# Splitting the value product of a fused FNet + SwiGLU kernel inside one accumulator bank, on ten of twelve units of a tile

## The chip, the cores and the metric

The kernel runs on one core of one Trainium2 chip. The metric is device time in microseconds (us) of one execution; the time of a kernel is the median over its timed runs. Beside the timed runs there is one profiled execution, whose trace gives every instruction of the five engines: PE (TensorE, the matmuls), DVE (VectorE), ACT (ScalarE), POOL (GpSimd) and SP (SyncE, which here only issues DMAs).

## The reference

```python
# x: (8, 3008, 256) float32; w_gate, w_val: (256, 1536); w_out: (1536, 256)
X = np.fft.fft(x, axis=1)
X = np.fft.fft(X, axis=2)
x = X.real.astype(np.float32).reshape(24064, 256)
g = x @ w_gate
silu = g * (1.0 / (1.0 + np.exp(-g)))
val = x @ w_val
out = (silu * val @ w_out).astype(np.float32)      # (24064, 256)
```

## The kernel before

The 24,064 rows of the Fourier transform come in mirrored pairs: row k and row M-k of a batch share an even part P (in the tile `Pt`) and an odd part Q (in `Qt`). The kernel never forms the rows. It multiplies P and Q with weights that hold the second Fourier transform already (`Wp`, `Wq`, and `Wm`, which is minus two times `Wq` in all rows but the first). So P·Wp + Q·Wq is the value for row k, and adding Q·Wm to that turns it into the value for the mirrored row. In the rest of this text "plus" is row k and "minus" is the mirrored row.

The 12,032 pairs lie in 24 tiles (`wide`): tiles 0 and 3 have 480 columns, tile 23 has 320, the others 512. Each tile has 12 units, one for each block of 128 hidden columns (`f`), so there are 288 units `(t, f)`, done in order by the loop at L954. A unit needs a gate and a value for both signs:

- `part_a(u)` (L761) opens a bank `g` of PSUM for the gate and adds P·Wp and Q·Wq into it (two matmuls, helper at L771).
- In a **whole** unit the value bank `v` gets the same two matmuls; ACT takes silu(g) into `sg` (L808), and DVE multiplies it with `v` into `hp`, the plus half of the hidden tile (L809). In the next unit, `part_b(prev)` (L812) adds Q·Wm to both banks (two matmuls, L818); ACT takes silu again (L826) and DVE multiplies into `hm`, reversed (L827). That is six matmuls, two silus and two DVE instructions.
- In a **split** unit the value bank `e` gets P·Wp alone. DVE adds the first row's term (L787: `es = bc*w0 + e`, `bc` being a broadcast of row 0 of Q). The inner function `odd()` (L789), run after four output matmuls of the same unit, puts Q·Wm into a second bank `o` (one matmul); DVE makes the plus value `es - o/2` into a buffer `VV` (L793) and the minus value `es + o/2`. POOL multiplies the plus value with silu(g) into `hp` (L800). In kind "P" the minus value goes into `VV` too, reversed (L796), and POOL makes `hm` (L823). In kind "H" the minus value stays in PSUM (L799) and DVE makes `hm` (L827). `part_b` then adds Q·Wm to the gate only. That is five matmuls, two silus, and for "P" three DVE and two POOL instructions, for "H" four DVE and one POOL.

`split(u)` (L754) looks the kind up in four tables. Tile 0 has no split unit, tile 1 five, tile 2 six, tiles 3 to 18 seven each (f = 0, 2, 10 of kind H; 4, 6, 8, 9 of kind P), tiles 19 to 22 eight each (all P), tile 23 seven.

Between these matmuls stand the output matmuls of the tile before (`OWork`, L707; L734): 96 of 256 columns for a 512-column tile, eight in each unit, in two groups of four. ACT copies their banks out (L694) and SP sends the rows. The next batches' P and Q are made in the same loop: POOL folds the input (L167 to L198, spread over the units by `seq`), and at two neighbouring units (f = 4 and 5 of a tile) `transform` (L579) runs matmuls into one `v` and one `g` bank, ACT copies one (L619), and DVE adds the two into `Pt` and `Qt` ("puts", L624).

PSUM has eight banks: three for `g`, three for `v` and `e`/`o` and the transform, two for the output. They come from rotating pools (L78 to L80), as do the SBUF buffers `sg` (3), `sgv` (4) and `es` (2); `VV` has four slots in turn. The order of the instructions on each engine is the order in which the code writes them.

Of the kernel before, what the change touches and what calls it, by code (L numbers as in the profile page):

```python
# [12 lines left out]
F32 = mybir.dt.float32  # L13
# [18 lines left out]
def kernel(  # L32
# [8 lines left out]
    nc = tc.nc  # L41
# [33 lines left out]
    cp = ctx.enter_context(tc.tile_pool(name="coef", bufs=2))  # L75
    pqp = ctx.enter_context(tc.tile_pool(name="pq", bufs=5))
    odp = ctx.enter_context(tc.tile_pool(name="od", bufs=2))
    psG = ctx.enter_context(tc.tile_pool(name="psG", bufs=3, space=bass.MemoryType.PSUM))  # L78
    psV = ctx.enter_context(tc.tile_pool(name="psV", bufs=3, space=bass.MemoryType.PSUM))
    psO = ctx.enter_context(tc.tile_pool(name="psO", bufs=2, space=bass.MemoryType.PSUM))  # L80
    ctx.enter_context(tc.manual_schedule())

    Wp = const.tile([P, 2, Dff], BF16, name="Wp")
    Wq = const.tile([P, 2, Dff], BF16, name="Wq")
# [494 lines left out]
    def transform(b, part, eos, given=None):  # L579
        n = NCE if part == 0 else G  # L580
        ev, ods = {}, {}
        ps = given or {eo: [pool.tile([P, T], F32, name=nm) for pool, nm in ((psV, "v"), (psG, "g"))] for eo in eos}

        def product(eo, kind, q, coef, r, qc, ch, start):
            CE, BB = coef
            if part == 0:
                cols = KINDS[kind][1]
                l, r_ = ce_main(CE, r, qc, eo, kind), Tab[r, ch, q, eo, cols]
            else:
                cols = slice(0, G)  # L590
                l, r_ = BB[r, qc, eo, kind, 0:P], Tab[r, ch, q, (eo + kind) % 2, NOO:NTAB]
            nc.tensor.matmul(ps[eo][q][:, cols], l, r_, start=start, stop=(ch == 1 and kind == 1), skip_group_check=True)  # L592

        if not given:
            every = slice(0, P)
            for eo in eos:
                for q in range(2):
                    for kind in range(2):
                        product(eo, kind, q, coef_a(b), every, q, 0, kind == 0)
                    if part == 0 and eo == 1:  # L600
                        row0(coef_a(b)[0], every, q, 0, q, ps[eo][q])
            for eo in eos:
                for kind in range(2):
                    for q in range(2):
                        if b == 0:
                            product(eo, kind, q, coef_c(b), every, q, 1, False)
                        else:
                            product(eo, kind, q, coef_c(b), half(q), b % 2, 1, False)
                if part == 0 and eo == 1:
                    for kind, cols in KINDS:  # L610
                        for q in range(2):
                            r = half(q)
                            nc.tensor.matmul(ps[eo][q][:, cols], ce_zero(coef_c(b)[0], r, b % 2, kind),
                                             Tab[r, 1, q, 0, cols], start=False, stop=True, skip_group_check=True)
        for q in range(2):
            for eo in eos:
                if q == 0:
                    ods[eo] = odp.tile([P, NCE], F32, name="od")
                    nc.scalar.copy(ods[eo][:, 0:n], ps[eo][q][:, 0:n])  # L619
                else:  # L620
                    ev[eo] = ps[eo][q]

        def put(eo, dst, s0, w, minus):
            nc.vector.tensor_tensor(dst, ev[eo][:, s0:s0 + w], ods[eo][:, s0:s0 + w],  # L624
                                    op=Alu.subtract if minus else Alu.add)

        if part == 0:
            runs = [(0, GH, 1, 0), (GH, GH, 0, 1), (G, GH, GH + 1, 0), (G + GH, GH, GH + 1, 1)]
        else:
            runs = [(2 * G, G, 0, 0), (3 * G, G, 0, 1)]  # L630
        todo = []
        for eo in eos:
            for c0, n_, s0, minus in runs:
                for t, off, src, w in pieces(b * H + c0, n_):
                    todo.append((t, eo, off, s0 + src, w, minus))
        for t, eo, off, s0, w, minus in sorted(todo, key=lambda v: v[0:2]):
            put(eo, pq_tiles(t)[eo][:, off:off + w], s0, w, minus)
        if part == 0:
            for eo in eos:
                put(eo, last[eo][:, b:b + 1], 0, 1, 0)  # L640
# [13 lines left out]


    hp = ctx.enter_context(tc.tile_pool(name="ht", bufs=2))
    sgp = ctx.enter_context(tc.tile_pool(name="sg", bufs=3))
    rdp = ctx.enter_context(tc.tile_pool(name="rd", bufs=2, space=bass.MemoryType.DRAM))
    sgv = ctx.enter_context(tc.tile_pool(name="sgv", bufs=4))
    esp = ctx.enter_context(tc.tile_pool(name="es", bufs=2))  # L660
    bcp = ctx.enter_context(tc.tile_pool(name="bc", bufs=2))

# [80 lines left out]
    owork = None  # L743

    ROW0 = (7, 9)
    SPLIT = {0: "H", 2: "H", 4: "P", 6: "P", 8: "P", 9: "P", 10: "H"}
    SPLIT_END = {0: "P", 1: "P", 3: "P", 4: "P", 6: "P", 8: "P", 9: "P", 11: "P"}
    SPLIT_1 = {2: "H", 4: "P", 6: "H", 8: "P", 10: "H"}
    SPLIT_2 = {0: "H", 2: "H", 4: "P", 6: "P", 8: "H", 10: "H"}
    t_end = tile_of((B - 1) * H) - 1  # L750

    bc = {}
# [1 line left out]
    def split(u):  # L754

        t, f = u
        if t == 0 or (t == nT - 1 and f > 9):
            return None
        return (SPLIT_1 if t == 1 else SPLIT_2 if t == 2 else SPLIT if t < t_end else SPLIT_END).get(f)

    def part_a(u):  # L761
        t, f = u
        n = width(t)
        w = n + (B if t == nT - 1 else 0)
        fs = slice(f * P, (f + 1) * P)
        if f == 0:
            hts[t] = (hp.tile([P, nF, T + B], BF16, name="hp"), hp.tile([P, nF, T], BF16, name="hm"))
        Pt, Qt = pq_tiles(t)

        def mm(ps, Wt, gv, src, start, stop):  # L770
            nc.tensor.matmul(ps[:, :w], Wt[:, gv, fs], src[:, :w], start=start, stop=stop,  # L771
                             skip_group_check=True)

        g = psG.tile([P, T], F32, name="g")
        mm(g, Wp, 0, Pt, True, False)
        if u == (0, 0):
            v = psV.tile([P, T], F32, name="v")
            mm(v, Wp, 1, Pt, True, False)
        mm(g, Wq, 0, Qt, False, True)
        if split(u):  # L780
            e = psV.tile([P, T], F32, name="v")
            mm(e, Wp, 1, Pt, True, True)
            sg = sgv.tile([P, T], F32, name="sgv")
            nc.scalar.activation(sg[:, :w], g[:, :w], AF.Silu)  # L784
            stt = nc.vector.scalar_tensor_tensor
            es = esp.tile([P, T], F32, name="es")
            stt(es[:, :w], bc[t][:, :w], w0[:, f:f + 1], e[:, :w], op0=Alu.mult, op1=Alu.add)  # L787

            def odd():  # L789
                o = psV.tile([P, T], F32, name="v")  # L790
                mm(o, Wm, 1, Qt, True, True)
                vp = next_of(VV, "vv")
                stt(vp[:, :w], o[:, :w], -0.5, es[:, :w], op0=Alu.mult, op1=Alu.add)  # L793
                if split(u) == "P":
                    vm = next_of(VV, "vv")
                    stt(vm[:, n - 1::-1], o[:, :n], 0.5, es[:, :n], op0=Alu.mult, op1=Alu.add)  # L796
                else:
                    vm = o
                    stt(o[:, :n], o[:, :n], 0.5, es[:, :n], op0=Alu.mult, op1=Alu.add)  # L799
                nc.gpsimd.tensor_tensor(hts[t][0][:, f, :w], sg[:, :w], vp[:, :w], op=Alu.mult)  # L800
                state[u] = (g, vm)
            return odd
        if u != (0, 0):
            v = psV.tile([P, T], F32, name="v")
            mm(v, Wp, 1, Pt, True, False)
        mm(v, Wq, 1, Qt, False, True)
        sg = sgp.tile([P, T], F32, name="sg")
        nc.scalar.activation(sg[:, :w], g[:, :w], AF.Silu)  # L808
        nc.vector.tensor_tensor(hts[t][0][:, f, :w], sg[:, :w], v[:, :w], op=Alu.mult)  # L809
        state[u] = (g, v)  # L810

    def part_b(u):  # L812
# [4 lines left out]
        for gv, ps in ((0, g), (1, v))[:1 if split(u) else 2]:  # L817
            nc.tensor.matmul(ps[:, :w], Wm[:, gv, f * P:(f + 1) * P], Qt[:, :w], start=False, stop=True,  # L818
                             skip_group_check=True)
        if split(u) == "P":  # L820
            sg = sgv.tile([P, T], F32, name="sgv")
            nc.scalar.activation(sg[:, w - 1::-1], g[:, :w], AF.Silu)  # L822
            nc.gpsimd.tensor_tensor(hts[t][1][:, f, :w], sg[:, :w], v[:, :w], op=Alu.mult)  # L823
            return
# [125 lines left out]
        nc.sync.dma_start(out=bc[t][:, :w], in_=row0d.pop(t)[0, :w].partition_broadcast(P))  # L950

    prev = None
    owork = None
    for i, u in enumerate(units):  # L954
        t, f = u
# [4 lines left out]
        for fn in before.pop(i, ()):  # L960
            fn()
        run_loads(i)
        odd = part_a(u)
        if owork:
            owork.run(4)
        if odd:
            odd()
        if prev is not None:
            part_b(prev)
            run_evicts()  # L970
# [50 lines left out]
```

## Time and profile before

| | |
|---|---|
| median of 3 timed runs | 655.53 us (655.26 to 655.82) |
| profiled execution | 654.94 us |
| its span, first to last instruction | 653.1 us |
| PE busy | 644.2 us (99%), 4319 matmuls |
| DVE busy | 561.2 us (86%), 1010 instructions |
| POOL busy | 538.5 us (82%), 554 instructions |
| ACT busy | 416.8 us (64%), 742 instructions |
| PE clock granted | 0.999 |

A group of instructions in the profile has a line of the kernel, an engine, an operation, `out<-in`, shapes, a count, then the busy time of all and the mean time of one. A line of the timeline has the start and the duration of one instruction, or of several equal ones, in microseconds. The duration of one instruction (its record) can overlap that of the next on the same engine, so the distance from start to start is told apart from it below.

### The profile page before, as it was taken

The numbers are of one execution on the slowest core, as the hardware profiler recorded it, in microseconds if no ns is written. First come the engines' busy times: TensorE is split into PE (matmuls) and PEld (weight loads), VectorE is DVE, ScalarE is ACT, GpSimd is POOL, SyncE is SP. The second block draws the span as 40 slices with busy tenths as digits, with TensorE's granted clock in tenths as the row PEclk, the third lists the DMA queues.
The fourth block names the chain that finished last, engine by engine and source line by source line (L and its number), as shares of the span: only waits on it lengthen the run. The fifth ranks groups of instructions, "written<-read, shape, count | busy, mean of one in ns | idle before, by whom it ended". The sixth has DMA issues, their size and how long they took to land.

```text
span 653.1 us, 13384 instructions
## 1 busy us (share of the span) xinstructions
PE 644.2 (99%) x4319; PEld 409.4 (63%) x4319; DVE 561.2 (86%) x1010; ACT 416.8 (64%) x742; POOL 538.5 (82%) x554
## 2 busy tenths in 40 slices
PE   9989999999999999999999999999999999999997
PEld 6446666666656666566666666666666666666686
DVE  8888888889889898898988988988988888888881
ACT  7676666666666666666666666666666666666663
POOL 9997987899689999995996988986788867877871
PEclk9999999999999999999999999999999999999999
DMA  9582324427213512154225211134111111111112
GB/s 230 110 179 61 90 77 121 144 83 158 81 58 98 147 55 76 56 120 134 61 80 139 80 42 50 56 78 127 57 46 45 43 47 46 54 34 57 55 49 74
DMA packets 52980, 55.42 MB, mean 85 GB/s; under 512 B 7504, under 2 KB 44238, under 8 KB 52910
## 3 DMA queue, kind: packets, MB, share of 16 engines
q1 hardware_dynamic: 49726, 52.20, 28.9%
q0 software_dynamic: 3184, 2.36, 2.5%
q8 instruction: 34, 0.56, 0.4%
q14 instruction: 36, 0.29, 0.2%
HBM read 32.22 MB, written 24.67 MB: 87 GB/s over the span
## 4 chain that ended last, share of the span: by engine, by line
PE 92%; DVE 2%; issue 0%; POOL 0%; ACT 0%; DVEq 0%; ACTq 0%
PE o L734 37%; PE v L771 19%; PE g L771 19%; PE g L818 9%; PE v L818 4%; PE v L592 3%; PE g L592 1%; DVE hm L827 0%; DVE hp L809 0%; PE o L453 0%; DVE VV L332 0%; POOL hp L800 0%; POOL hm L823 0%; PE v L573 0%; PE g L573 0%
## 5 line engine op out<-in xcount | busy, mean ns | idle before, releaser
L800 POOL TENSOR_TENSOR hp<-sgv,VV 128x512 bf16<-128x512 f32 (+2 forms) x162 | 203.6, 1257 | 76.6 <-DVE VV L793 67.4
L734 PE MATMUL o<-Wo,hp 128*128 128x256 bf16 (+2 forms) x1140 | 169.6, 273 | 0.0
L734 PE MATMUL o<-Wo,hm 128*128 128x256 bf16 (+2 forms) x1140 | 169.6, 273 | 0.0
L826 ACT ACTIVATE sg<-g 128x512 f32<-128x512 f32 (+2 forms) x181 | 107.0, 591 | 75.1 <-PE g L818 51.5
L734 PEld LDWEIGHTS <-hm 128*128 128x128 bf16 (+2 forms) x1140 | 112.0, 98 | 64.3 <-issue 0.2
L734 PEld LDWEIGHTS <-hp 128*128 128x128 bf16 (+2 forms) x1140 | 112.0, 98 | 62.9
L823 POOL TENSOR_TENSOR hm<-sgv,VV 128x512 bf16<-128x512 f32 (+2 forms) x107 | 132.8, 1247 | 12.6 <-ACT sgv L822 12.0
L787 DVE SCALAR_TENSOR_TENSOR es<-bc,w,v 128x512 f32<-128x512 bf16 (+2 forms) x162 | 118.8, 733 | 15.5 <-PE v L771 15.3
L827 DVE TENSOR_TENSOR hm<-sg,v 128x512 bf16<-128x512 f32 (+2 forms) x181 | 121.7, 672 | 10.7 <-ACT sg L826 10.2
L793 DVE SCALAR_TENSOR_TENSOR VV<-v,es 128x512 f32<-128x512 f32 (+2 forms) x162 | 110.5, 682 | 22.4 <-POOL hp L800 1.2
L784 ACT ACTIVATE sgv<-g 128x512 f32<-128x512 f32 (+2 forms) x162 | 96.4, 595 | 39.5 <-PE g L771 32.9
L771 PE MATMUL g<-Pt,Wp 128*128 128x512 bf16 (+2 forms) x288 | 108.2, 376 | 0.1
L771 PE MATMUL g<-Qt,Wq 128*128 128x512 bf16 (+2 forms) x288 | 107.9, 375 | 0.3 <-DVE Qt L624 0.3
L771 PE MATMUL v<-Pt,Wp 128*128 128x512 bf16 (+2 forms) x288 | 107.9, 375 | 0.1
L818 PE MATMUL g<-Qt,Wm 128*128 128x512 bf16 (+2 forms) x288 | 107.8, 374 | 0.0
L822 ACT ACTIVATE sgv<-g 128x512 f32<-128x512 f32 (+2 forms) x107 | 62.8, 587 | 53.8 <-PE g L818 45.5
L809 DVE TENSOR_TENSOR hp<-sg,v 128x512 bf16<-128x512 f32 (+2 forms) x126 | 84.4, 670 | 4.8 <-ACT sg L808 4.5
L808 ACT ACTIVATE sg<-g 128x512 f32<-128x512 f32 (+2 forms) x126 | 74.3, 590 | 21.3 <-PE g L771 18.5
L771 PEld LDWEIGHTS <-Wp 128*128 128x128 bf16 x576 | 56.2, 98 | 43.1 <-issue 6.6
L796 DVE SCALAR_TENSOR_TENSOR VV<-v,es 128x512 f32<-128x512 f32 (+2 forms) x107 | 71.4, 668 | 2.6 <-POOL hm L823 2.6
L771 PE MATMUL v<-Qt,Wm 128*128 128x512 bf16 (+2 forms) x162 | 60.6, 374 | 0.2 <-DVE hm L827 0.2
L694 ACT COPY EV<-o 128x512 f32<-128x512 f32 x90 | 52.2, 581 | 4.8 <-PE o L734 4.8
(173 smaller groups left out, 683.8 us busy)
## 6 DMA issues: line engine op xcount, KB each, us to landing
out_dram<-EV SPq DMA_DIRECT2D x96, 128.0 KB
XA<-in_x_dram SPq DMA_DIRECT2D x32, 256.0 KB
XA<-in_x_dram SPq DMA_DIRECT2D x112, 64.0 KB
XC<-in_x_dram SPq DMA_DIRECT2D x210, 16.0 KB
XC<-in_x_dram SPq DMA_DIRECT2D x56, 60.0 KB
bc<-row SPq DMA_DIRECT2D x20, 128.0 KB
out_dram<-EV SPq DMA_DIRECT2D x12, 120.0 KB
out_dram<-EV SPq DMA_DIRECT2D x10, 112.0 KB
```

Source lines behind the costliest of these rows:

```text
L734: nc.tensor.matmul(ps[:n, j, :], hts[minus][:, f, c:c + n], Wo[:, f, :], start=(f == 0), stop=(f == nF - 1))
L771: nc.tensor.matmul(ps[:, :w], Wt[:, gv, fs], src[:, :w], start=start, stop=stop, skip_group_check=True)
L784: nc.scalar.activation(sg[:, :w], g[:, :w], AF.Silu)
L787: stt(es[:, :w], bc[t][:, :w], w0[:, f:f + 1], e[:, :w], op0=Alu.mult, op1=Alu.add)
L793: stt(vp[:, :w], o[:, :w], -0.5, es[:, :w], op0=Alu.mult, op1=Alu.add)
L800: nc.gpsimd.tensor_tensor(hts[t][0][:, f, :w], sg[:, :w], vp[:, :w], op=Alu.mult)
L808: nc.scalar.activation(sg[:, :w], g[:, :w], AF.Silu)
L809: nc.vector.tensor_tensor(hts[t][0][:, f, :w], sg[:, :w], v[:, :w], op=Alu.mult)
L818: nc.tensor.matmul(ps[:, :w], Wm[:, gv, f * P:(f + 1) * P], Qt[:, :w], start=False, stop=True, skip_group_check=True)
L823: nc.gpsimd.tensor_tensor(hts[t][1][:, f, :w], sg[:, :w], v[:, :w], op=Alu.mult)
L826: nc.scalar.activation(sg[:, :w], g[:, :w], AF.Silu)
L827: nc.vector.tensor_tensor(hts[t][1][:, f, w - 1::-1], sg[:, :w], v[:, :w], op=Alu.mult)
```

## The change

A split unit keeps its value in one bank. `part_a` puts P·Wp into `e` as before, and DVE takes `es` from it as before. The odd part is then added onto the same bank: `odd()` adds Q·Wq (not Q·Wm), so that `e` becomes the plus value itself. DVE multiplies it with silu(g) into `hp` directly from PSUM; the minus value is `2*es - e`, written reversed into `VV`, and POOL makes `hm`. There is one kind of split unit.

`odd()` of a unit is run one unit later, behind `part_a` and four output matmuls of the next unit and ahead of its own `part_b`. Ten units of a tile are split instead of seven (tiles 4 to 18: all but f = 2 and 8), eleven in tiles 19 to 22 (all but 5), seven in tile 1, nine in tiles 2, 3 and 23, none in tile 0. The six banks of `g` and `v` are no longer pools, but fixed tiles in a line that is passed on by hand: a unit takes the first and puts it at the end; `transform` takes the first and puts it at the second place (`aside`), so it is the next but one to be taken. `sg` has four buffers and `sgv` three.

```diff
+    class Banks:
+        def __init__(self, nm):
+            self.line = [psB.tile([P, T], F32, name=f"{nm}{i}") for i in range(3)]
+        def tile(self, shape=None, dt=None, name=None, aside=False):
+            b = self.line.pop(0)
+            self.line.insert(1 if aside else 2, b)
+            return b if shape is None or len(shape) == 2 else b.rearrange("p (q d) -> p q d", q=shape[1])
+    psG, psV = Banks("g"), Banks("v")
...
-        ps = given or {eo: [pool.tile([P, T], F32, name=nm) for pool, nm in ((psV, "v"), (psG, "g"))] for eo in eos}
+        ps = given or {eo: [pool.tile(aside=True) for pool in (psV, psG)] for eo in eos}
...
-    SPLIT = {0: "H", 2: "H", 4: "P", 6: "P", 8: "P", 9: "P", 10: "H"}
-    SPLIT_END = {0: "P", 1: "P", 3: "P", 4: "P", 6: "P", 8: "P", 9: "P", 11: "P"}
-    SPLIT_1 = {2: "H", 4: "P", 6: "H", 8: "P", 10: "H"}
-    SPLIT_2 = {0: "H", 2: "H", 4: "P", 6: "P", 8: "H", 10: "H"}
+    WHOLE = {0: range(nF), 1: (0, 3, 5, 7, 9), 2: (2, 6, 10), 3: (2, 6, 10)}
+    WHOLE_MID, WHOLE_END = (2, 8), (5,)
...
         if split(u):
             e = psV.tile([P, T], F32, name="v")
-            mm(e, Wp, 1, Pt, True, True)
-            sg = sgv.tile([P, T], F32, name="sgv")
+            mm(e, Wp, 1, Pt, True, False)
+            sg = sgp.tile([P, T], F32, name="sg")
...
             def odd():
-                o = psV.tile([P, T], F32, name="v")
-                mm(o, Wm, 1, Qt, True, True)
-                vp = next_of(VV, "vv")
-                stt(vp[:, :w], o[:, :w], -0.5, es[:, :w], op0=Alu.mult, op1=Alu.add)
-                if split(u) == "P":
-                    vm = next_of(VV, "vv")
-                    stt(vm[:, n - 1::-1], o[:, :n], 0.5, es[:, :n], op0=Alu.mult, op1=Alu.add)
-                else:
-                    vm = o
-                    stt(o[:, :n], o[:, :n], 0.5, es[:, :n], op0=Alu.mult, op1=Alu.add)
-                nc.gpsimd.tensor_tensor(hts[t][0][:, f, :w], sg[:, :w], vp[:, :w], op=Alu.mult)
+                mm(e, Wq, 1, Qt, False, True)
+                nc.vector.tensor_tensor(hts[t][0][:, f, :w], sg[:, :w], e[:, :w], op=Alu.mult)
+                vm = next_of(VV, "vv")
+                stt(vm[:, n - 1::-1], es[:, :n], 2.0, e[:, :n], op0=Alu.mult, op1=Alu.subtract)
                 state[u] = (g, vm)
...
-        odd = part_a(u)
+        coming = part_a(u)
         if owork:
             owork.run(4)
         if odd:
             odd()
+        odd = coming
         if prev is not None:
             part_b(prev)
```

More of the change, by code (lines that the diff above doesn't have):

```diff
@@ L77 @@
     odp = ctx.enter_context(tc.tile_pool(name="od", bufs=2))
-    psG = ctx.enter_context(tc.tile_pool(name="psG", bufs=3, space=bass.MemoryType.PSUM))
-    psV = ctx.enter_context(tc.tile_pool(name="psV", bufs=3, space=bass.MemoryType.PSUM))
+    psB = ctx.enter_context(tc.tile_pool(name="psB", bufs=1, space=bass.MemoryType.PSUM))
     psO = ctx.enter_context(tc.tile_pool(name="psO", bufs=2, space=bass.MemoryType.PSUM))
     ctx.enter_context(tc.manual_schedule())
+    class Banks:
[6 more added lines that the diff above has]
+    psG, psV = Banks("g"), Banks("v")
     Wp = const.tile([P, 2, Dff], BF16, name="Wp")
@@ L656 @@
     hp = ctx.enter_context(tc.tile_pool(name="ht", bufs=2))
-    sgp = ctx.enter_context(tc.tile_pool(name="sg", bufs=3))
+    sgp = ctx.enter_context(tc.tile_pool(name="sg", bufs=4))
     rdp = ctx.enter_context(tc.tile_pool(name="rd", bufs=2, space=bass.MemoryType.DRAM))
-    sgv = ctx.enter_context(tc.tile_pool(name="sgv", bufs=4))
+    sgv = ctx.enter_context(tc.tile_pool(name="sgv", bufs=3))
     esp = ctx.enter_context(tc.tile_pool(name="es", bufs=2))
@@ L756, in split @@
         t, f = u
-        if t == 0 or (t == nT - 1 and f > 9):
-            return None
-        return (SPLIT_1 if t == 1 else SPLIT_2 if t == 2 else SPLIT if t < t_end else SPLIT_END).get(f)
+        if t == nT - 1 and f > 9:
+            return False
+        return f not in WHOLE.get(t, WHOLE_MID if t < t_end else WHOLE_END)
     def part_a(u):
@@ L786, in part_a @@
             es = esp.tile([P, T], F32, name="es")
-            stt(es[:, :w], bc[t][:, :w], w0[:, f:f + 1], e[:, :w], op0=Alu.mult, op1=Alu.add)
+            stt(es[:, :n], bc[t][:, :n], w0[:, f:f + 1], e[:, :n], op0=Alu.mult, op1=Alu.add)
             def odd():
-                o = psV.tile([P, T], F32, name="v")
-                mm(o, Wm, 1, Qt, True, True)
-                vp = next_of(VV, "vv")
-                stt(vp[:, :w], o[:, :w], -0.5, es[:, :w], op0=Alu.mult, op1=Alu.add)
-                if split(u) == "P":
-                    vm = next_of(VV, "vv")
-                    stt(vm[:, n - 1::-1], o[:, :n], 0.5, es[:, :n], op0=Alu.mult, op1=Alu.add)
-                else:
-                    vm = o
-                    stt(o[:, :n], o[:, :n], 0.5, es[:, :n], op0=Alu.mult, op1=Alu.add)
-                nc.gpsimd.tensor_tensor(hts[t][0][:, f, :w], sg[:, :w], vp[:, :w], op=Alu.mult)
+                mm(e, Wq, 1, Qt, False, True)
+                nc.vector.tensor_tensor(hts[t][0][:, f, :w], sg[:, :w], e[:, :w], op=Alu.mult)
+                vm = next_of(VV, "vv")
+                stt(vm[:, n - 1::-1], es[:, :n], 2.0, e[:, :n], op0=Alu.mult, op1=Alu.subtract)
                 state[u] = (g, vm)
@@ L819, in part_b @@
                              skip_group_check=True)
-        if split(u) == "P":
+        if split(u):
             sg = sgv.tile([P, T], F32, name="sgv")
@@ L952 @@
     prev = None
+    odd = None
     owork = None
```

## The prediction

> **What bounds the kernel now.** I read the head of the page first (span, engines), then one answer of the windows over the long middle, then the chain that ended last, then what PE waits for, then the timeline of two units, then the groups by form.
>
> ```profile
> span 653.1 us, 13384 instructions
> PE 644.2 (99%) x4319; PEld 409.4 (63%) x4319; DVE 561.2 (86%) x1010; ACT 416.8 (64%) x742; POOL 538.5 (82%) x554
> ...
> 60.00:620.00 560.00, 559.80 (x3746) 354.25 (x3745) 494.05 (x860) 358.59 (x635) 470.55 (x446) 1.00 0.29 79
> ...
> PE 92%; DVE 2%; issue 0%; POOL 0%; ACT 0%; DVEq 0%; ACTq 0%
> PE o L734 37%; PE v L771 19%; PE g L771 19%; PE g L818 9%; PE v L818 4%; PE v L592 3%; PE g L592 1%; DVE hm L827 0%; DVE hp L809 0%; PE o L453 0%; DVE VV L332 0%; POOL hp L800 0%; POOL hm L823 0%; PE v L573 0%; PE g L573 0%
> ...
> PE v L818 <- DVE hp L809: 2.3, 3, 1.9
> PE o L289 <- DVE sel L244: 1.0, 1, 1.0
> ```
>
> From 60 to 620 us PE is idle for 560.00 - 559.80 = 0.2 us, at the full clock (1.00). The chain is 92% PE, and the longest sum of waits on PE is 2.3 us. So in the middle the time is the number of matmuls times their spacing, as long as the other engines stay ahead. A busy PE alone would not prove that, since its ends are modelled; the start times do, in the next fence.
>
> ```profile
> 302.64 0.38 PE L771 MATMUL v<-Pt,Wp 128*128 128x512 bf16 x1
> ...
> 303.17 0.74 DVE L787 SCALAR_TENSOR_TENSOR es<-bc,w,v 128x512 f32<-128x512 bf16 x1
> ...
> 306.33 0.38 PE L771 MATMUL g<-Pt,Wp 128*128 128x512 bf16 x1
> ...
> 306.55 0.38 PE L771 MATMUL g<-Qt,Wq 128*128 128x512 bf16 x1
> ...
> 306.72 0.69 DVE L793 SCALAR_TENSOR_TENSOR VV<-v,es 128x512 f32<-128x512 f32 x1
> 306.76 0.38 PE L771 MATMUL v<-Pt,Wp 128*128 128x512 bf16 x1
> ...
> 306.98 0.60 PE L734 MATMUL o<-Wo,hm 128*128 128x256 bf16 x4
> ...
> 307.33 0.68 DVE L796 SCALAR_TENSOR_TENSOR VV<-v,es 128x512 f32<-128x512 f32 x1
> 307.41 0.38 PE L771 MATMUL v<-Qt,Wm 128*128 128x512 bf16 x1
> ...
> 307.63 0.38 PE L818 MATMUL g<-Qt,Wm 128*128 128x512 bf16 x1
> 307.63 0.53 PEld L734 LDWEIGHTS <-hm 128*128 128x128 bf16 x4
> 307.85 0.60 PE L734 MATMUL o<-Wo,hm 128*128 128x256 bf16 x4
> 307.93 0.74 DVE L787 SCALAR_TENSOR_TENSOR es<-bc,w,v 128x512 f32<-128x512 bf16 x1
> ...
> 308.28 0.38 PE L771 MATMUL g<-Pt,Wp 128*128 128x512 bf16 x1
> ...
> 308.80 0.69 DVE L793 SCALAR_TENSOR_TENSOR VV<-v,es 128x512 f32<-128x512 f32 x1
> ```
>
> This is one split unit. From start to start a 512-column matmul takes 0.215 us (306.33, 306.55, 306.76), though its record says 0.38. Four output matmuls take 0.43 (306.98 to 307.41). The unit is 308.28 - 306.33 = 1.95 us; a whole unit has one more 512-column matmul, so 2.165.
>
> The same lines price DVE. Where the next instruction does not need the one ahead of it, starts lie 0.61 and 0.60 apart (306.72, 307.33, 307.93) while the records are 0.69 and 0.68: a record overlaps the next by 0.08. Where it does need it (L793 reads the `es` that L787 has just written), the start comes 0.87 after (307.93 to 308.80), 0.13 more than the 0.74 of the record.
>
> **The change, part by part.** *Fewer matmuls.* A split unit has five matmuls of full width before and after: `o<-Qt,Wm` becomes `e<-Qt,Wq`. What changes the sum is the number of split units: 162 before (5 in tile 1, 6 in tile 2, 7 in each of 16, 8 in each of 4, 7 in the last), 228 after (7, 9, 9 in tile 3, 10 in each of 15, 11 in each of 4, 9). That is 66 matmuls fewer: 62 of 512 columns, two of 480 in tile 3, two of 328 in the last. At 0.215 us, scaled by columns for the small ones, 62 x 0.215 + 2 x 0.20 + 2 x 0.14 = 14.0 us. Their weight loads go as well; in the steady part loads hide under matmuls.
>
> *DVE.* The groups by form, in 512 columns:
>
> ```profile
> L800 POOL TENSOR_TENSOR hp<-sgv,VV 128x512 bf16<-128x512 f32 x148 | 188.9, 1277 | 70.8 <-DVE VV L793 62.3 <-ACT sg L808 6.3 <-ACT sgv L784 1.3
> L823 POOL TENSOR_TENSOR hm<-sgv,VV 128x512 bf16<-128x512 f32 x96 | 122.0, 1277 | 11.9 <-ACT sgv L822 11.2 <-DVE hp L809 0.4
> L787 DVE SCALAR_TENSOR_TENSOR es<-bc,w,v 128x512 f32<-128x512 bf16 x148 | 110.0, 743 | 14.1 <-PE v L771 13.8
> L827 DVE TENSOR_TENSOR hm<-sg,v 128x512 bf16<-128x512 f32 x156 | 106.3, 681 | 8.9 <-ACT sg L826 8.4
> L809 DVE TENSOR_TENSOR hp<-sg,v 128x512 bf16<-128x512 f32 x104 | 70.9, 682 | 0.6 <-ACT sg L808 0.4 <-PE g L818 0.2
> L796 DVE SCALAR_TENSOR_TENSOR VV<-v,es 128x512 f32<-128x512 f32 x96 | 65.5, 682 | 1.8 <-POOL hm L823 1.8
> ```
>
> Every new instruction has a twin here: `es` 743 ns, `hp` from `sg` and PSUM 682 (as L809), the reversed minus value 682 (as L796). A split unit's records are 2.107 us. By starts the order of a steady unit is `es` of this unit, then `hp` and minus value of the last one. `hp` does not need that `es`: 0.743 - 0.08 = 0.66. Minus value after `hp`: 0.60. The next `es` is the awkward one. There are two `es` buffers, and with `odd` a unit late it overwrites the one that the minus value, the instruction right ahead of it, reads. In the built program 121 of the 228 `es` wait for an earlier DVE instruction, six of ten in a tile without a transform. I price those at 0.68 + 0.13 = 0.81, from the dependent pair above, and the others at 0.61. Tiles 4 to 18 are twice five split units and a whole one: 5 x 0.66 + 5 x 0.60 + 3 x 0.81 + 2 x 0.61, and for the whole unit's two products 2 x 0.60: 11.15 us. PE needs 5 x 1.95 + 2.165 = 11.92 for the six. DVE falls behind by about 0.1 us in some units and makes it up at the whole one.
>
> [...] The sum goes by the starts; a rival below takes whole records.
>
> *The new wait on PE.* `e<-Qt,Wq` must wait for `es`, which reads the same bank; queued behind it on PE are the gate's last matmul and all output matmuls. In unit time (first gate matmul at 0) `e` starts at 0.43 and `es` 0.53 later (302.64 to 303.17), ending at 0.96 + 0.74 = 1.70. The odd part comes at 1.95 + 0.65 + 0.43 = 3.03. The cover is 1.3 us; a DVE that is late by less costs nothing. A bank must be free again three units after it was taken; its last reader ends about 1.4 us ahead of that. So in the steady part: no stall.
>
> *At a transform* the cover is thinner:
>
> ```profile
> 294.05 0.33 PE L592 MATMUL v<-Tab,CEa 128*128 128x189 bf16 x2
> ...
> 294.75 0.39 PE L771 MATMUL g<-Pt,Wp 128*128 128x512 bf16 x1
> ...
> 295.51 1.33 DVE L624 TENSOR_TENSOR Pt<-g,od 128x64 bf16<-128x64 f32 x7
> ...
> 296.71 0.33 PE L592 MATMUL v<-Tab,CEa 128*128 128x189 bf16 x2
> 296.74 0.68 DVE L809 TENSOR_TENSOR hp<-sg,v 128x512 bf16<-128x512 f32 x1
> ...
> 298.05 0.39 PE L771 MATMUL g<-Pt,Wp 128*128 128x512 bf16 x1
> ...
> 268.29 0.54 PE g L771 x2
> ...
> 346.65 0.54 PE g L771 x2
> ```
>
> The first transform takes PE 0.70 (294.05 to 294.75), the second 1.34 (296.71 to 298.05); the puts hold DVE 1.23 (295.51 to 296.74), starting 0.76 after the next unit. Follow unit u, whose time is 0, with transforms behind u and u+1: unit u+1 starts at 1.95 + 0.70 = 2.65; puts 3.41 to 4.64; `es` of u+1 to 5.30; `hp` of u to 5.90; minus value of u, whole record, to 6.58. PE: second transform 4.60 to 5.94, `e` of u+2 at 6.37, and the bank line gives it the bank of u. So PE stalls about 0.2 us there; where the puts start earlier it is nothing. Fourteen transform pairs stand among split units; at 0 to 0.2 each I take 0.1, together 1.4 us, in a range from 0 to 14 x 0.6 = 8.4 (every pair late by a further 0.4).
>
> *POOL* no longer makes `hp` and makes every split unit's `hm`: 228 products instead of 162 + 107 (the kind P), about 41 x 1.277 = 52 us less in all, and in a middle tile 12.8 us instead of 14.0. Its folds stay where they are. `VV` is used once a unit instead of twice, so its four slots reach further; `sgv` loses a buffer but is also used once a unit. Cost nothing; the cover is POOL's smaller load. *ACT* keeps its count: nothing. *SP* issues the same DMAs in the same places. The first 60 us and the last 13, in which PE waits for the start-up or runs output matmuls alone, hold few of the units that change: between -0.5 and +1, taken as 0.
>
> *Sum.* 654.94 (profiled execution) - 14.0 + 1.4 = 642.3. The median before lies 0.59 above the profiled execution (655.53 against 654.94): 642.9.
>
> **The rivals.** *DVE becomes the bound because records do not overlap.* By whole records a middle tile needs 10 x 2.107 + 2 x 1.363 = 23.8, puts four times 1.33 in three tiles = 1.8, and six dependent gaps of 0.13: 26.4 us. PE has (346.65 - 268.29) / 3 = 26.12 a tile now (three tiles lie between these two transforms), 25.47 after. That is 0.9 over in each of 15 tiles and, with eleven splits, about 2.2 over in each of 4: 22 us, so 665 and slower. It passes the time before once DVE needs some 0.2 us more in a split unit than I worked out. Against it: starts 0.60 apart; by starts the tile is 22.3 + 4 x 1.23 / 3 = 23.9, 6% below PE. For it: six percent is little, and 228 units multiply any slip.
>
> *Stalls at the transforms and banks eat a part.* The 8.4 us bound above instead of 1.4: 649.9. For it: the 0.2 us that I find is the difference of two long sums, and the second `e` bank is gone. Against: in the rows before, DVE never holds PE by more than 1.9 us at a time.
>
> *Fewer splits help PE nowhere.* If PE were held by something that the trace hides, 66 matmuls would give nothing: 655.5. The spacing of 0.215 with no gap speaks against it.
>
> **How the numbers follow.** Forecast (640.5 to 645): 0.68. Stalls eat a part (645 to 651): 0.17. DVE-bound, slower: 0.10. Nothing: 0.02. Better than 640.5, from the start-up: 0.03. The range 640.5 to 651 holds 0.85, leaving out the DVE-bound case. A measurement of this kernel can tell 0.2% (1.3 us) from no change; faster by more 0.88, same 0.02, slower 0.10.
>
> **What would show it.** Right: 66 matmuls fewer and PE near 644.2 - 14.0 = 630 us at 98 or 99%; a PE unit of 1.95; DVE starts 0.66, 0.60 and 0.61 or 0.81 apart; POOL near 538.5 - 52 = 486 us; PE waits for DVE only at f = 6 behind the transforms. Wrong: many short waits of PE at `e<-Qt,Wq` or at the first `e` matmul in every tile (DVE-bound), or POOL late so that ACT waits for `sgv`.

## The result and the profile after

The changed kernel takes 649.70 us (median of 4 runs, 649.44 to 651.37) against 655.39 us for the kernel before beside it: a ratio of 0.9919 (95% interval 0.9901 to 0.9938). The forecast was 642.9. The sign was right, and the time lies inside the range given, but less than half of the forecast gain of 12.6 us came, and for a reason that was none of the rivals.

The head of the page after, its chain by engine, and the longest of PE's own waits with the wait of ACT that belongs to it (who waited, for whom, us in total, times, longest):

```profile
span 647.7 us, 13099 instructions
PE 625.0 (96%) x4183; PEld 403.1 (62%) x4253; DVE 566.3 (87%) x1021; ACT 415.9 (64%) x742; POOL 491.2 (76%) x513
...
PE 88%; DVE 5%; POOL 2%; ACT 1%; issue 1%; DMA 1%; SPq 0%; DVEq 0%; ACTq 0%
...
ACT sg L812 <- POOL BBc L552: 13.2, 1, 13.2
PE g L822 <- ACT sg L812: 11.0, 1, 11.0
PE v L782 <- DVE VV L804: 1.7, 6, 0.3
```

PE has 4253 weight loads, 66 fewer than 4319, as forecast. (70 matmul records are missing from this trace, so PE's busy time and its gaps are read with care here; the starts that are shown below are records.) POOL, forecast at 486, has 491.2. What DVE's minus value costs PE in the waits is 1.7 us in six places. But one wait, once, is 11.0 us, and POOL now stands on the chain. It lies in the start-up:

```profile
25.89 0.37 PE L782 MATMUL v<-Qt,Wq 128*128 128x480 bf16 x1
...
34.83 1.18 POOL L552 TENSOR_SCALAR BBc<-EOf,sgn 128x128 bf16<-128x128 f32 x3
36.10 0.50 POOL L552 TENSOR_SCALAR BBc<-SC,sgn 128x1 bf16<-128x1 f32 x2
36.64 0.57 ACT L812 ACTIVATE sg<-g 128x480 f32<-128x480 f32 x1 [13.19 <-POOL BBc L552]
...
37.26 0.56 PE L822 MATMUL g<-Qt,Wm 128*128 128x480 bf16 x1 [11.00 <-ACT sg L812]
```

The first silu of the kernel, in unit (0, 0), starts at 36.64 us, right behind the last start-up instruction of POOL that reads `SC`. It has no data from POOL. In the trace of before the same silu starts at 24.93:

```profile
24.93 0.57 ACT L808 ACTIVATE sg<-g 128x480 f32<-128x480 f32 x1 [1.09 <-DMA XC<-in_x_dram]
...
48.70 0.38 PE L936 MATMUL o<-Qt,sel 128*128 128x512 bf16 x1
```

The last row is the first matmul of tile 1, the first tile that has a split unit. After the change it comes at 59.75:

```profile
59.75 0.38 PE L940 MATMUL o<-Qt,sel 128*128 128x512 bf16 x1
```

So the two spans can be cut there. Up to tile 1 the changed kernel loses 59.75 - 48.70 = 11.05 us. From tile 1 to the end it takes 647.7 - 59.75 = 587.95 us instead of 653.1 - 48.70 = 604.40: it gains 16.45, more than forecast. The difference, 5.4, is that of the spans. Two things were thus to be explained: the start-up, and 16.45 instead of 12.6.

### The profile page after: what moved, and what is told of

Its sections match the earlier page's. It is cut to its first block, busy times and chain, and to the rows that moved or that the text cites. A ratio compares the mean times of both kernels' runs of the same rounds, so it can differ in the third digit from the quotient of the medians.

```text
span 647.7 us, 13099 instructions
## 1 busy us (share of the span) xinstructions
PE 625.0 (96%) x4183; PEld 403.1 (62%) x4253; DVE 566.3 (87%) x1021; ACT 415.9 (64%) x742; POOL 491.2 (76%) x513
## 4 chain that ended last, share of the span: by engine, by line
PE 88%; DVE 5%; POOL 2%; ACT 1%; issue 1%; DMA 1%; SPq 0%; DVEq 0%; ACTq 0%
PE o L747 37%; PE v L782 19%; PE g L782 16%; PE g L822 9%; PE v L605 2%; PE v L822 2%; DVE hp L802 1%; PE g L605 1%; DMA XA<-in_x_dram 1%; DVE Pt L637 1%; DVE VV L804 1%; DVE hp L813 1%; DVE es L798 1%; ACT sg L812 1%; POOL BBc L552 0%
## 5 line engine op out<-in xcount | busy, mean ns | idle before, releaser
L827 POOL TENSOR_TENSOR hm<-sgv,VV 128x512 bf16<-128x512 f32 (+2 forms) x228 | 286.4, 1259 | 124.8 <-DVE VV L804 97.5
L826 ACT ACTIVATE sgv<-g 128x512 f32<-128x512 f32 (+2 forms) x228 | 134.6, 590 | 126.9 <-PE g L822 119.5
L798 DVE SCALAR_TENSOR_TENSOR es<-bc,w,v 128x512 f32<-128x512 bf16 (+2 forms) x228 | 167.6, 735 | 13.9 <-DMA bc<-row 1.0
L802 DVE TENSOR_TENSOR hp<-sg,v 128x512 bf16<-128x512 f32 (+2 forms) x228 | 152.9, 671 | 0.5 <-PE g L822 0.3
L804 DVE SCALAR_TENSOR_TENSOR VV<-es,v 128x512 f32<-128x512 f32 (+2 forms) x228 | 152.8, 670 | 0.0
L782 PE MATMUL v<-Qt,Wq 128*128 128x512 bf16 (+2 forms) x285 | 107.0, 375 | 0.0
L782 PE MATMUL g<-Qt,Wq 128*128 128x512 bf16 (+2 forms) x224 | 83.9, 375 | 0.3 <-DVE Qt L637 0.3
L782 PEld LDWEIGHTS <-Wq 128*128 128x128 bf16 x576 | 56.5, 98 | 15.3 <-issue 3.0
L813 DVE TENSOR_TENSOR hp<-sg,v 128x512 bf16<-128x512 f32 (+2 forms) x60 | 39.9, 666 | 22.2 <-ACT sg L812 21.6
L831 DVE TENSOR_TENSOR hm<-sg,v 128x512 bf16<-128x512 f32 (+2 forms) x60 | 40.1, 668 | 17.9 <-ACT sg L830 17.8
L822 PEld LDWEIGHTS <-Wm 128*128 128x128 bf16 x348 | 34.1, 98 | 17.7 <-POOL BBc L552 11.3
```

The source lines that it names most:

```text
L798: stt(es[:, :n], bc[t][:, :n], w0[:, f:f + 1], e[:, :n], op0=Alu.mult, op1=Alu.add)
L802: nc.vector.tensor_tensor(hts[t][0][:, f, :w], sg[:, :w], e[:, :w], op=Alu.mult)
L804: stt(vm[:, n - 1::-1], es[:, :n], 2.0, e[:, :n], op0=Alu.mult, op1=Alu.subtract)
```

## The experiments

**What holds up the start-up.** The start-up's scratch tiles are freed at L653 of the kernel before, and the pools of the main loop are laid over that memory. Read from the built programs: three `sg` buffers cover the bytes 206048 to 212192 of a partition, the fourth 212192 to 214240; the scratch tile `SA` begins at 213440 and `SC` behind it at 221632. With three buffers `sg` lies over a filler tile (`pad`) that nothing reads; with four it reaches 800 bytes into `SA`, which POOL reads until about 28 us, in one pool with `SC`, read until 36.6. The first silu then has to wait until POOL has done 62 instructions instead of 34 (the count in its wait on POOL's semaphore), although its own buffer, the first of the four, overlaps neither tile. Three kernels test that. The first makes the filler 2048 bytes longer, which moves `SA` and `SC` up and changes no instruction (the silu's count is 34 again):

```diff
-    tp.tile([P, 1900], F32, name="pad")
+    tp.tile([P, 2412], F32, name="pad")
```

> The changed kernel with the filler in the start-up's scratch memory 2048 bytes longer, so that the four sg buffers no longer overlap the tiles SA and SC of the start-up; no instruction and no order changes. In the changed kernel the first silu waited 13.2 us for POOL's last reading of those tiles and PE stood 11.0 us behind it. Theory (the fourth sg buffer was laid over that memory): the silu starts near 25 us as before, the 11 us go, 649.7 - 11 = 638.7 us, with PE's sum of waits under 6 us. Rival (POOL or the banks passed on by hand hold up the start-up whatever the addresses): 648 to 651 us and the wait still there.

Measured: 638.53 us, ratio to before 0.9756 (0.9738 to 0.9773). The first silu and the first matmul of tile 1, then PE's waits:

```profile
24.16 0.57 ACT L812 ACTIVATE sg<-g 128x480 f32<-128x480 f32 x1 [1.09 <-DMA XC<-in_x_dram]
...
47.10 0.38 PE L940 MATMUL o<-Qt,sel 128*128 128x512 bf16 x1
...
PE v L822 <- DVE hp L813: 1.6, 3, 1.2
PE v L782 <- DVE VV L804: 1.4, 5, 0.4
PE v L782 <- DVE es L798: 1.2, 1, 1.2
```

The silu no longer waits for POOL, and tile 1 begins 12.65 us sooner. An address alone was worth about 11 us of 650 (649.70 - 638.53). The second kernel goes back to the pool sizes of before and keeps the rest of the change:

```diff
-    sgp = ctx.enter_context(tc.tile_pool(name="sg", bufs=4))
+    sgp = ctx.enter_context(tc.tile_pool(name="sg", bufs=3))
-    sgv = ctx.enter_context(tc.tile_pool(name="sgv", bufs=3))
+    sgv = ctx.enter_context(tc.tile_pool(name="sgv", bufs=4))
```

> The changed kernel with three sg and four sgv buffers, as the kernel before has them; everything else is the change. Theory (memory overlap): about 638.7 us as with the longer filler; if a split unit needed the fourth sg buffer, some more, up to 645. Rival (banks by hand or the order of the start-up): 648 to 651 us.

Measured: 639.73 us, 0.9769 (0.9752 to 0.9786). Four `sg` and three `sgv` buffers, which cost the 11 us at that address, bring nothing over three and four that the intervals can tell from zero. The third puts the four and three buffers into the kernel before and nothing else:

```diff
-    sgp = ctx.enter_context(tc.tile_pool(name="sg", bufs=3))
+    sgp = ctx.enter_context(tc.tile_pool(name="sg", bufs=4))
-    sgv = ctx.enter_context(tc.tile_pool(name="sgv", bufs=4))
+    sgv = ctx.enter_context(tc.tile_pool(name="sgv", bufs=3))
```

> The kernel before with four sg and three sgv buffers and nothing else of the change. Theory (memory overlap): the first silu waits about 12 us for POOL here too, 655.4 + 11 = 666 us. Rival (the stall needs the new banks or the new split): 655 to 656 us. A lack of sgv buffers in the kernel before, whose split units of kind P take two, could add up to 3 us later on.

Measured: 673.67 us, 1.029 (1.0268 to 1.0311). Its waits:

```profile
PE g L818 <- ACT sg L808: 11.7, 1, 11.7
PE g L771 <- ACT sgv L822: 3.3, 4, 1.4
...
ACT sgv L822 <- POOL hp L800: 26.5, 29, 2.8
```

The stall appears without a line of the split or of the banks: 11.7 us at the same place. The time is 8 us above the forecast 666. The likely reason is that the old split, which uses `sgv` twice in a unit of kind P, is short of buffers with three (ACT's wait for POOL there is 26.5 us; it was 8.2 in before); 3.3 us of that reach PE in the row above, and the rest of the 8 is not assigned. The changed split runs as well with three as with four (638.53 and 639.73), so the pool sizes need not have been touched.

**Where 16 us come from.** The next kernel has the longer filler and as many split units as before (162 in all, with 7 in the last tile; the matmul count is that of before):

```diff
-    WHOLE = {0: range(nF), 1: (0, 3, 5, 7, 9), 2: (2, 6, 10), 3: (2, 6, 10)}
-    WHOLE_MID, WHOLE_END = (2, 8), (5,)
+    WHOLE = {0: range(nF), 1: (0, 1, 3, 5, 7, 9, 11), 2: (1, 3, 5, 7, 9, 11)}
+    WHOLE_MID, WHOLE_END = (1, 3, 5, 7, 11), (2, 5, 7, 10)
```

> The changed kernel with the longer filler, and with as many split units as the kernel before: 5, 6, 7, 7 in tiles 1 to 3 and in the middle, 8 in tiles 19 to 22 (7 in the last tile became 9, since the table of the last tiles is used there too, less the two unsplit at the end: f = 0, 1, 3, 4, 6, 8, 9). Same count of matmuls as before, but value and odd part in one bank, POOL relieved. If the whole gain is the 66 matmuls: 638.7 + 14.0 = 652.7 us or up to the 655.4 of before. If the one-bank split is worth something by itself beyond its matmuls: under 652 us. If it costs stalls: above 656.

Measured: 650.18 us, 0.9931 (0.9912 to 0.995), and 638.53 with the longer filler and 228 splits, run beside it. The one-bank split is worth 4.3 us without a matmul less; the 66 matmuls are worth another 11.7. The profiles from tile 1 to the end agree: 604.4 us before, 600.1 here (648.4 - 48.34), 589.0 with the longer filler (636.1 - 47.10), so 4.3 and 11.1. Part of the 4.3 shows in the starts: in the kernel before, the odd part of unit f = 0 comes 0.48 us after the first of the four output matmuls ahead of it, here the next matmul comes after 0.43, the bare spacing. Before, then this one:

```profile
283.89 0.69 DVE L827 TENSOR_TENSOR hm<-sg,v 128x512 bf16<-128x512 f32 x1
...
284.15 0.60 PE L734 MATMUL o<-Wo,hm 128*128 128x256 bf16 x4
...
284.63 0.38 PE L771 MATMUL v<-Qt,Wm 128*128 128x512 bf16 x1
```

```profile
282.12 0.60 PE L747 MATMUL o<-Wo,hm 128*128 128x256 bf16 x4
282.55 0.38 PE L822 MATMUL g<-Qt,Wm 128*128 128x512 bf16 x1
```

Such a gap of 0.05 stands at f = 0, 2 and 4 of a middle tile: about 2.4 us over 16 tiles, an estimate (48 x 0.05). Whether the kind of the unit makes it was asked of the kernel before with the kinds moved:

```diff
-    SPLIT = {0: "H", 2: "H", 4: "P", 6: "P", 8: "P", 9: "P", 10: "H"}
+    SPLIT = {0: "P", 2: "P", 4: "P", 6: "H", 8: "H", 9: "P", 10: "H"}
```

> The kernel before with the same number of split units of each kind in tiles 3 to 18, but f = 0 and 2 of kind P and f = 6 and 8 of kind H. In the trace of before, the units f = 0 and 2 take 2.21 us and f = 6 and 8, with the same six matmuls, 2.17. If kind H makes the 0.05 (its two banks are held longer), f = 0 and 2 go to 2.17 and f = 6 and 8 to 2.21, and the time stays near 654.5. If the place makes it (POOL, or the first units of a tile), f = 0 and 2 stay at 2.21. POOL's order changes too, which could cost up to 3 us.

Measured: 668.5 us, 1.0189 (1.0162 to 1.0217), slower by far more than expected. The first three rows are of f = 8, now of kind H, in tile 11, the next two of f = 9, the last three of f = 0, now of kind P, in tile 12:

```profile
333.77 0.69 DVE L827 TENSOR_TENSOR hm<-sg,v 128x512 bf16<-128x512 f32 x1 [0.30 <-ACT sg L826]
...
334.03 0.60 PE L734 MATMUL o<-Wo,hm 128*128 128x256 bf16 x4
...
334.51 0.38 PE L771 MATMUL v<-Qt,Wm 128*128 128x512 bf16 x1
...
336.46 0.68 DVE L827 TENSOR_TENSOR hm<-sg,v 128x512 bf16<-128x512 f32 x1
...
337.19 0.38 PE L771 MATMUL v<-Qt,Wm 128*128 128x512 bf16 x1 [0.35 <-DVE hm L827]
...
342.48 0.69 DVE L827 TENSOR_TENSOR hm<-sg,v 128x512 bf16<-128x512 f32 x1
...
342.73 0.60 PE L734 MATMUL o<-Wo,hm 128*128 128x256 bf16 x4
...
343.22 0.38 PE L771 MATMUL v<-Qt,Wm 128*128 128x512 bf16 x1
```

The gap stayed at f = 0, went from f = 2 and 4 (units of 2.17 us instead of 2.21 by their starts) and came to f = 8. So a unit's own kind does not make it. What the units with this gap have in common, in both kernels, is that the split unit two places back, with a whole one between, is of kind H. In the built programs the odd part of such a unit gets the bank `o` in which that unit of kind H keeps its minus value, and its `hm` reads it late: it ends at 283.89 + 0.69 = 284.58 in before, at 334.46 and 343.17 here, and the odd part comes 0.05 behind each. One bank a unit does away with that wait. The slowdown comes from f = 8 to 10: the odd part at 337.19 has the bank of the whole unit f = 7 and waits for its `hm` (336.46 + 0.68), which DVE reaches only then. The split with two banks is touchy here about which kinds stand near each other. The rest of the 4.3 us, beyond these gaps, was not broken down.

**Is the bank line needed, and the late odd part?** Both with the longer filler. First the transform's bank put at the end of the line:

```diff
-        ps = given or {eo: [pool.tile(aside=True) for pool in (psV, psG)] for eo in eos}
+        ps = given or {eo: [pool.tile() for pool in (psV, psG)] for eo in eos}
```

> The changed kernel with the longer filler (638.5 us), in which a transform puts the bank that it takes at the end of the line, as a unit does, and not aside. By the walk through a transform pair the second transform would then take the bank of the unit between them two places back, whose minus value is made at 6.6 us where PE wants the bank at 4.6: 1.9 us of stall in each of 14 pairs, 27 us, so about 665 us. If DVE has more slack there than the walk says: 638 to 645 us.

Measured: 678.71 us, 1.0367 (1.0344 to 1.0389).

```profile
309.98 0.33 PE L605 MATMUL v<-Tab,CEa 128*128 128x189 bf16 x2 [1.71 <-DVE VV L804]
...
PE v L605 <- DVE VV L804: 21.0, 14, 1.7
PE v L782 <- DVE VV L804: 7.6, 12, 0.8
```

The second transform waits for the minus value, 14 times, up to 1.71 us (worked out: 1.9); 7.6 us that I had not foreseen follow at the units behind it, since the late transform makes DVE late again. The place in the line at which a transform puts its bank back is thus worth 40 us (678.71 - 638.53); the listed waits for the minus value make 28.6 of them, and the forecast had 27. Then the odd part in its own unit:

```diff
-        coming = part_a(u)
+        odd = part_a(u)
         if owork:
             owork.run(4)
         if odd:
             odd()
-        odd = coming
```

> The changed kernel with the longer filler, in which odd() runs in its own unit again, four output matmuls behind part_a, while value and odd part share one bank. PE then comes to the odd part at 0.43 + 0.215 + 0.43 = 1.08 us of the unit, and es, which it has to wait for, ends at 1.70: 0.6 to 0.7 us of stall in each of 228 split units, 140 to 160 us, so 780 to 800 us. If PE's wait on es costs little, since DVE runs ahead: below 660.

Measured: 798.32 us, 1.2194 (1.2167 to 1.222).

```profile
401.86 0.75 DVE L798 SCALAR_TENSOR_TENSOR es<-bc,w,v 128x512 f32<-128x512 bf16 x1
...
402.66 0.38 PE L782 MATMUL v<-Qt,Wq 128*128 128x512 bf16 x1 [0.40 <-DVE es L798]
...
PE v L782 <- DVE es L798: 124.9, 228, 1.4
```

Every one of the 228 odd parts waits for its `es`. Sharing the bank is only affordable here because `odd()` comes a unit later.

**How close DVE is.** With the longer filler, a third `es` buffer:

```diff
-    esp = ctx.enter_context(tc.tile_pool(name="es", bufs=2))
+    esp = ctx.enter_context(tc.tile_pool(name="es", bufs=3))
```

> The changed kernel with the longer filler and three es buffers instead of two, so that es no longer overwrites what the minus value right ahead of it reads (12 es wait for DVE in the program, not 121). That frees 0.2 us of DVE in about half of the split units. If DVE's lag costs PE nothing but what the transforms show: 637.5 to 638.7. If DVE bounds the kernel: 630 to 635.

Measured: 638.35 us, 0.9751 (0.9732 to 0.977): no difference to 638.53. In the starts the dependent gap is gone: 0.79 from minus value to `es` in the changed kernel, 0.60 here. Changed kernel, then this one:

```profile
311.04 0.75 DVE L798 SCALAR_TENSOR_TENSOR es<-bc,w,v 128x512 f32<-128x512 bf16 x1
311.71 0.68 DVE L802 TENSOR_TENSOR hp<-sg,v 128x512 bf16<-128x512 f32 x1
312.30 0.68 DVE L804 SCALAR_TENSOR_TENSOR VV<-es,v 128x512 f32<-128x512 f32 x1
313.09 0.75 DVE L798 SCALAR_TENSOR_TENSOR es<-bc,w,v 128x512 f32<-128x512 bf16 x1
```

```profile
256.63 0.68 DVE L804 SCALAR_TENSOR_TENSOR VV<-es,v 128x512 f32<-128x512 f32 x1
257.23 0.74 DVE L798 SCALAR_TENSOR_TENSOR es<-bc,w,v 128x512 f32<-128x512 bf16 x1
```

DVE got faster and the kernel did not: DVE was off the path, but for waits too small to show in the medians. Then more splits, first eleven in the middle tiles with two `es` buffers:

```diff
-    WHOLE_MID, WHOLE_END = (2, 8), (5,)
+    WHOLE_MID, WHOLE_END = (8,), (5,)
```

> The changed kernel with the longer filler and eleven split units in tiles 4 to 18 too (whole: f = 8 alone). 15 matmuls fewer, 3.2 us: 635.3 if DVE keeps up. By starts DVE needs 25.0 us a tile and PE 25.1, so it stands at the edge: 637 to 641 if the lag at the transforms is no longer made up by f = 2.

Measured: 637.03 us, 0.9742 (0.9718 to 0.9767): 1.5 of the 3.2 us, at the lower edge of the second case, and the interval overlaps with that of ten splits. Two places show where the rest stays, the first in tile 4 (`es`, the odd part that waits for it, the next `es`), the second behind a first transform (the gate's second and the value's first matmul):

```profile
130.76 0.75 DVE L798 SCALAR_TENSOR_TENSOR es<-bc,w,v 128x512 f32<-128x512 bf16 x1
...
131.56 0.38 PE L782 MATMUL v<-Qt,Wq 128*128 128x512 bf16 x1
...
132.80 0.75 DVE L798 SCALAR_TENSOR_TENSOR es<-bc,w,v 128x512 f32<-128x512 bf16 x1
...
287.25 0.38 PE L782 MATMUL g<-Qt,Wq 128*128 128x512 bf16 x1
...
287.77 0.38 PE L782 MATMUL v<-Pt,Wp 128*128 128x512 bf16 x1
```

With two `es` buffers DVE needs 2.04 us from `es` to `es`, more than PE's 1.95. In tile 4 it has just been held up by the DMA of `bc` (1.37 us), and with f = 2 split it stays behind: five units go at its pace, 2.04 or 2.05 us each, until the whole unit f = 8. Behind the transform the two matmuls are 0.52 instead of 0.215 apart, the second right behind a minus value that ends at 287.71. The same with three `es` buffers:

> Longer filler, eleven split units in tiles 4 to 18, three es buffers. If DVE is still off the path: 636 to 637, as with two es buffers (637.0). If the es buffers were what kept eleven from its full 3.2 us: 635.

Measured: 635.94 us, 0.971 (0.9693 to 0.9726), lower than with two buffers, though the intervals overlap; it lies between the two expected cases and decides for neither. And all twelve, three buffers (35 matmuls fewer than with ten, since the table also turns one narrow unit of the last tile):

```diff
-    WHOLE_MID, WHOLE_END = (2, 8), (5,)
+    WHOLE_MID, WHOLE_END = (), ()
-    esp = ctx.enter_context(tc.tile_pool(name="es", bufs=2))
+    esp = ctx.enter_context(tc.tile_pool(name="es", bufs=3))
```

> Longer filler, all twelve units of tiles 4 to 22 split, three es buffers: no whole unit is left for DVE to catch up in. Against ten and eleven splits 34 matmuls fewer, 7.3 us: 631 if DVE keeps up (by starts 12 x 1.87 + 1.6 = 24.0 us a tile against 24.9 on PE). If the lag that the transforms leave is never made up, PE waits at every unit behind them: 636 to 645, with waits of PE on DVE of 10 us or more.

Measured: 632.84 us, 0.9662 (0.964 to 0.9683), the fastest here: 5.7 us below ten splits, where 7.3 were to be had.

```profile
PE 616.3 (98%) x4148; PEld 400.0 (63%) x4218; DVE 586.6 (93%) x1056; ACT 411.7 (65%) x742; POOL 532.6 (84%) x548
...
PE v L782 <- DVE VV L804: 1.0, 4, 0.3
...
PE v L782 <- DVE es L798: 0.7, 1, 0.7
```

DVE is 93% busy and costs PE 1.7 us in these waits, 0.7 of them where `es` itself had waited for the DMA of `bc`. A middle tile has no whole unit left, and DVE, with three `es` buffers, still keeps up.

## Why the prediction was right or wrong

- **The step that failed** is the start-up term: "hold few of the units that change: between -0.5 and +1, taken as 0". It measured +11.05 us. I had looked there for changed units and not for changed memory. Under POOL the `sgv` pool was weighed by how many buffers the loop needs, and the `sg` pool not at all; that a fourth `sg` buffer must lie somewhere, and over what, was not asked. The kernel says it at L653 and in a filler of 1900 elements at L367 that nothing reads. That the time still fell into the range is luck: without the stall it is 638.53, below the range, which the prediction had at a chance of 0.03.
- **Fewer matmuls:** 66, right. Their worth less the stalls was put at 14.0 - 1.4 = 12.6; between the kernels with 162 and 228 splits it measured 650.18 - 638.53 = 11.7. One wait of 1.2 us for `es`, which itself had waited for the DMA of `bc`, stands in the profile with 228 splits and not in that with 162.
- **The mis-sized term** is the split itself. I took its five matmuls to cost the same before and after, and it measured 4.3 us less. The 1.95 us came from one unit, f = 10 of tile 10 behind another split unit, the good case of the kernel before; the units behind a whole one and at the transforms were not compared, and the gaps of 0.05 stood in the trace.
- **DVE by starts:** `es` to `hp` 0.66 priced, 0.67 measured (311.04 to 311.71); `hp` to minus value 0.60 and 0.59; minus value to `es` 0.81 and 0.79. The records-do-not-overlap rival (665 us) is out: DVE has 566.3 us busy and PE waits 1.7 us on it. The minus value starts 0.59 after an `hp` whose record is 0.68. The `es` that needs the minus value ahead of it to be done, for its buffer, starts 0.79 after the start of that one, 0.11 behind the end of its record (312.30 + 0.68 = 312.98); with a third `es` buffer it starts 0.60 after the start of the minus value (256.63 to 257.23).
- **Transforms:** priced at 1.4 us in all; the waits of PE on the minus value list 1.4 us in the kernel with the longer filler, in five places and not fourteen, so the sum is right and its spread is not. The time landed in the interval of the "stalls eat a part" rival, but its mechanism had no part in it.
- **The new wait on PE:** cover of 1.3 us, and right but for the 1.2 us wait above; without the delay 124.9 us in 228 units, 0.55 in the mean.

## What to carry to other kernels

A buffer more in a pool is a placement as well as a count: where pools are laid over freed start-up memory, look up the addresses before and after, and what the first user of the pool must wait for. When a change sums well in the steady part, cut both traces at the first event that the change should touch and compare the two sides separately; here -16.45 and +11.05 hid in -5.4. A shared accumulator bank cost next to nothing here with a whole unit of other matmuls as cover for its reader (PE waits 1.2 us on `es`), and 160 us without (798.32 - 638.53).

## What the hardware showed

After its 11 us of waiting PE did not come back at full speed: its granted clock was 0.50. From 23 to 40 us the mean granted clock is 0.68, in the trace of before 1.00. The windows of the changed kernel (PE's granted clock is the third figure from the end):

```profile
37.00:38.00 1.00, 0.61 (x2) 0.16 (x2) 0.76 (x2) 1.00 (x3) 0.00 (x0) 0.50 0.68 179
...
40.00:41.00 1.00, 1.00 (x4) 0.45 (x3) 0.59 (x1) 0.75 (x2) 0.00 (x0) 0.50 0.51 123
...
42.00:43.00 1.00, 1.00 (x4) 0.40 (x3) 0.72 (x2) 0.75 (x2) 0.00 (x0) 0.60 0.49 133
43.00:44.00 1.00, 1.00 (x6) 0.49 (x5) 1.00 (x3) 1.00 (x3) 0.00 (x0) 1.00 0.53 145
```

The clock is 0.50 up to about 42.8 us, 5.5 us after PE resumed at 37.26 (an estimate: 0.8 us at 0.50 and 0.2 us at 1.00 make the mean of 0.60 from 42 to 43). What that cost is not shown: tile 1 comes 12.65 us later than with the longer filler, 1.65 more than the wait, but in the eleven kernels here without the stall it begins anywhere between 47.10 and 49.98, and 47.10 is that of the longer filler.
